# Another stated instruction order for attention and the first MLP, with the ring place of every tile stated

## The chip, the cores and the metric

The kernel runs on one core of one Trainium2 chip. The metric is device time in microseconds (us), the median of several executions. A profile is one execution recorded by the hardware; its span is shorter than its time by what lies around it. Engines are named as in the profile: PE (TensorE matmul), PEld (its weight loads), DVE (VectorE), ACT (ScalarE), POOL (GpSimd) and SP (SyncE, which here issues all DMAs).

## The reference, cut to what matters

Three parts follow one another: attention over 4 x 8 heads with a memory term, an MLP with a squared ReLU, and an MLP with a softmax-weighted activation and a layer norm.

```python
# attention: B, H, S, D = 4, 8, 576, 64
scores = scale * q @ k.T; scores = where(causal, -1e9, scores); scores -= scores.max(-1)
a = exp(scores); a /= a.sum(-1) + 1e-9
local = a @ v
q_p = phi(q)                      # phi(x) = where(x > 0, x, exp(x) - 1) + 1
mem_out = (q_p @ M_prev) / (q_p @ z_prev + 1e-6)
g = 1 / (1 + exp(-beta))          # one number for each head
x = g * mem_out + (1 - g) * local # -> 2304 tokens x 512
# MLP 1: d_ff 2048
r = maximum(x @ w_in, 0); x = (s * r * r + b) @ w_out
# MLP 2: d_ff 1024
h = x @ w_in2; solu = h * softmax(h); out = (layernorm(solu) * g_ln) @ w_out2
```

## The kernel before, in words

**Attention** works on 16 units (u = 0 to 15), each a pair of heads of one batch. The class `Attention` has one method for each step:

- `load` (L323): DMAs of keys and queries (`kq`), `q`, `v`, and once per batch `zb` and `Mb`.
- `scores` (L406): the score products of a unit in four groups, chunks 0 and 1 together (`s{u}_0`), then 2, 3 and 4 (`s{u}_2`, `s{u}_3`, `s{u}_4`). The products at L421 use 64 rows and all 128 columns of the PE array, those of group 4 (L452) the full array. DVE then takes scores and mask, writes `pr` and the row maximum `mx` (L437), and ACT takes the exponential with its row sum (L404). The scores have one buffer (`ps_s`), so the next group waits until DVE has read the one before.
- `transposes` (L463): PE transposes `pr` into `pp` (L478), ACT writes it scaled to `pt` (L482), for chunk 4 to `ptl`.
- `phi`, `weigh`, `recip_t`, `phi_t` (L343 to L400): the memory term's factors, transposed on PE as `tr`, `tp` and `tq` (L384, L394, L398).
- `values` (L493): products with `v`. `po` (L513) takes `pt_0` and then `pt_1`, `pe` (L516) takes `ptl`; both use all 128 rows and 64 columns of the array. `Mb` products on the full array end both (L518, L519).

**The first MLP** is spread over attention. Four of its 16 blocks of hidden units run there as filler (`first_part`, L566): hidden products `h` at L532 to L534, in `hidden`, and output products `y` at L594 to L596, all on the full array. The other 12 blocks run behind attention (`second_part`, ten rounds, L737 to L739), and then the second MLP (`mlp2`). Weights arrive as raw 8-byte numbers (`raw`, L246) and are decoded by ACT and DVE.

**What sets the order.** The text of the program gives a first order. `state_order` (L101) chains the instructions of each engine by the table `ORDER`, whose entries are indices into the program's text order, with `a+n` for a run of n. So each engine's queue from the start of the program to the first rounds of `second_part` is stated by hand; behind the stated part the order is that of the framework's scheduler. `load_gate` (L176) loads `beta` and makes `gate`, `omg` and `gmt` (ACT at L178, DVE at L179 to L185); `load_consts` (L187) loads `s_sb`, `b_sb` and `gl_sb`. `warm_up` (L170) issues products of zeros.

**Tiles.** A pool with `bufs=n` is a ring of n buffers for each tag. Before, the framework chooses which place of the ring a tile takes.

Of the kernel before, what the change touches and what calls it, by code (L numbers as in the profile page):

```python
# [15 lines left out]
PSUM = bass.MemoryType.PSUM  # L16
# [7 lines left out]

ORDER = {
    "PE": """
# [26 lines left out]
""",  # L53
    "Activation": """
# [15 lines left out]
""",  # L70
    "DVE": """
# [16 lines left out]
""",  # L88
    "Pool": """
3 15 17 5 11 0 13 2 6 12 8 10 14 16 20 18+2 23 21+2 26 24+2 29 27 32 28 30 35 31 33+2 38 36+2 41 39+2 44 42+2 47  # L90
45+2 50 48+2 53 51+2 56 54+2 59 57+2 60+2
""",
    "SP": """
# [3 lines left out]
""",  # L97
}


def state_order(tc):  # L101
    traced = {}
# [13 lines left out]
def attention_mlp_kernel(  # L116
# [76 lines left out]
    FP1 = 4  # L193
# [749 lines left out]
```

## Time and profile before

| | us |
|---|---|
| time, median of 3 runs (829.14 to 829.52) | 829.26 |
| the profiled execution: time | 829.67 |
| the profiled execution: span | 827.5 |
| PE busy in the span | 814.1 |
| ACT busy | 551.9 |
| DVE busy | 533.7 |
| POOL busy | 117.2 |

Read it like this: the profiled execution took 2.17 us more than its span and 0.41 us more than the median. Matmuls are pipelined and their ends are modelled, so on PE the distance from one start to the next tells more than the busy time of one instruction. The x in a timeline row counts hardware records: at L421, L452 and L513 to L519 one product of the program is two records, elsewhere it is one.

### The profile page before, as it was taken

The page shows a single profiled execution, that of the slowest core. Times are in us where ns is not written, and L with a number is a line of the kernel's source. Part 1 is how long each engine was busy: PE and PEld are TensorE (multiplying, and loading weights), DVE is VectorE, ACT ScalarE, POOL GpSimd, SP SyncE. Part 2 cuts the span into 40 slices and gives each one's busy share as a digit, 9 for nine tenths or more (in the row PEclk, how much of TensorE's full clock was granted, in tenths as well). Part 3 has the DMA queues.
Part 4 walks back from the last instruction along what each step waited for, and adds up shares of the span by engine and source line. Part 5 has one row for each costly group of instructions (what it writes and reads, how often), then busy time and mean ns, then how long its engine had stood idle before and what let it go on. Part 6 is the DMA issues. An engine that isn't in the chain of part 4 may idle for free.

```text
span 827.5 us, 13276 instructions
## 1 busy us (share of the span) xinstructions
PE 814.1 (98%) x4930; PEld 656.9 (79%) x4930; DVE 533.7 (64%) x1305; ACT 551.9 (67%) x1134; POOL 117.2 (14%) x124
## 2 busy tenths in 40 slices
PE   8999999999999999999999999999999999999997
PEld 6777777777777688888898888889887888888875
DVE  4999977978766566544566425454789665566552
ACT  6998878879778747666577656666865444445432
POOL 3221111111211100000000200030112233332000
PEclk9999999999999999999999999999999999999999
DMA  8342744343642025721132302211210000000001
GB/s 256 130 158 73 249 139 146 133 140 130 213 153 69 36 89 196 271 77 51 51 129 101 103 1 77 65 37 61 71 48 0 26 27 26 13 27 26 26 24 40
DMA packets 39759, 76.35 MB, mean 92 GB/s; under 512 B 6160, under 2 KB 16400, under 8 KB 39696
## 3 DMA queue, kind: packets, MB, share of 16 engines
q1 hardware_dynamic: 39696, 75.52, 27.2%
q8 instruction: 39, 0.64, 0.3%
q14 instruction: 24, 0.20, 0.1%
HBM read 61.35 MB, written 14.16 MB: 91 GB/s over the span
## 4 chain that ended last, share of the span: by engine, by line
PE 91%; DVE 4%; ACT 2%; DMA 1%; POOL 1%; issue 1%; SPq 0%; DVEq 0%; POOLq 0%
PE h L532 8%; PE h L533 8%; PE h L534 8%; PE y L738 6%; PE y L739 6%; PE y L737 6%; PE pp L478 5%; PE s L421 5%; PE o L871 4%; PE o L869 4%; PE o L870 4%; PE po L513 4%; PE y L596 2%; PE y L594 2%; PE y L595 2%; PE s L452 2%
## 5 line engine op out<-in xcount | busy, mean ns | idle before, releaser
L533 PE MATMUL h<-xl,w 128*128 128x512 f32 (+1 forms) x320 | 118.9, 372 | 0.0
L534 PE MATMUL h<-xh,w 128*128 128x512 f32 (+1 forms) x320 | 118.4, 371 | 0.0
L532 PE MATMUL h<-xh,w 128*128 128x512 f32 (+1 forms) x320 | 117.7, 378 | 0.0
L535 ACT ACTIVATE r<-h 128x512 f32<-128x512 f32 (+1 forms) x80 | 43.2, 553 | 90.6 <-PE h L534 87.8
L540 DVE TENSOR_TENSOR g<-r,g 128x512 fp32r<-128x512 f32 (+1 forms) x60 | 39.6, 665 | 83.4 <-ACT r L539 83.3
L738 PE MATMUL y<-g,w 128*128 128x512 f32 (+1 forms) x240 | 87.2, 368 | 0.0
L737 PE MATMUL y<-g,w 128*128 128x512 f32 (+1 forms) x240 | 87.2, 368 | 0.0
L404 ACT ACTIVATE pr<-pr,mx 128x512 f32<-128x512 f32 (+3 forms) x128 | 70.8, 555 | 16.1 <-DVE mx L437 15.6
L533 PEld LDWEIGHTS h<-xl,w 128*128 128x128 f32 x320 | 60.3, 189 | 10.8 <-DVE xl L562 1.1
L534 PEld LDWEIGHTS h<-xh,w 128*128 128x128 f32 x320 | 60.3, 189 | 10.2 <-DVE w L279 0.6
L532 PEld LDWEIGHTS h<-xh,w 128*128 128x128 f32 x320 | 59.7, 189 | 10.9 <-ACT r L535 0.6
L739 PE MATMUL y<-g,w 128*128 128x512 f32 (+1 forms) x240 | 66.6, 368 | 0.0
L437 DVE CUSTOM_DVE_ANT_0 pr<-s,big 128x128 f32<-128x128 f32 (+3 forms) x128 | 57.1, 487 | 14.5 <-PE s L421 12.6
L482 ACT ACTIVATE pt<-pp,omg 128x512 f32<-128x512 f32 (+3 forms) x128 | 60.1, 524 | 7.8 <-PE pp L478 7.3
L871 PE MATMUL o<-w,zl 128*128 128x512 f32 x144 | 56.6, 393 | 0.8 <-DVE var L847 0.8
L869 PE MATMUL o<-w,zh 128*128 128x512 f32 x144 | 56.7, 394 | 0.3 <-ACT zh L863 0.3
L870 PE MATMUL o<-w,zh 128*128 128x512 f32 x144 | 56.1, 390 | 0.0
L737 PEld LDWEIGHTS y<-g,w 128*128 128x128 f32 x240 | 45.3, 189 | 7.5
L421 PEld LDWEIGHTS s<-kq 64*128 64x128 f32 x640 | 39.7, 187 | 14.5 <-issue 7.2
L738 PEld LDWEIGHTS y<-g,w 128*128 128x128 f32 x240 | 45.2, 189 | 7.5
L478 PE MATMUL pp<-ident,pr 128*128 128x128 f32 x320 | 48.8, 276 | 2.2 <-ACT pr L404 2.1
L421 PE MATMUL s<-kq 64*128 64x128 f32 x640 | 48.6, 287 | 0.8 <-DVE mx L437 0.5
(165 smaller groups left out, 1855.7 us busy)
## 6 DMA issues: line engine op xcount, KB each, us to landing
raw<-in_moe_w_in_dram SPq DMA_DIRECT2D x24, 512.0 KB, 4.5
raw<-in_moe_w_out_dram SPq DMA_DIRECT2D x24, 512.0 KB, 3.7
kq<-in_kq_dram SPq DMA_DIRECT2D x16, 608.0 KB, 4.7
xr<-xd SPq DMA_DIRECT2D x8, 1024.0 KB, 5.4
q<-in_q_dram SPq DMA_DIRECT2D x16, 320.0 KB, 4.4
v<-in_v_dram SPq DMA_DIRECT2D x16, 320.0 KB, 3.4
xd<-xb SPq DMA_DIRECT2D x4, 1152.0 KB, 5.0
out_dram<-os SPq DMA_DIRECT2D x18, 256.0 KB, 2.0
```

The lines of the kernel that those rows point to most:

```text
L404: mark[0] = nc.scalar.activation(pr, pr, AF.Exp, bias=mx, scale=-1.0, accum_out=sm).ins
L421: self.last = nc.tensor.matmul(ss[:, j, c0 + k * P:c0 + (k + 1) * P], x[:, S + i * P:S + (i + 1) * P], x[:, k * P:(k + 1) * P], start=True ...
L478: nc.tensor.transpose(pp[:, e * n + c * P:e * n + (c + 1) * P], pr[:, c * P:(c + 1) * P], ident)
L532: nc.tensor.matmul(ps, wc[0], xh[:, c, 0:n], start=(c == 0), stop=False)
L533: nc.tensor.matmul(ps, wc[0], xl[:, c, 0:n], start=False, stop=False)
L534: nc.tensor.matmul(ps, wc[1], xh[:, c, 0:n], start=False, stop=(c == NC - 1))
L737: nc.tensor.matmul(o, wc[0], gh[:, 0:n], start=(f == fs[0]), stop=False)
L738: nc.tensor.matmul(o, wc[1], gh[:, 0:n], start=False, stop=False)
L739: nc.tensor.matmul(o, wc[0], gl[:, 0:n], start=False, stop=(f == fs[-1]))
L869: nc.tensor.matmul(oo, zh, w[:, 0], start=(f == 0), stop=False)
L870: nc.tensor.matmul(oo, zh, w[:, 1], start=False, stop=False)
L871: nc.tensor.matmul(oo, zl, w[:, 0], start=False, stop=(f == NF2 - 1))
```

## The change

`ORDER` is replaced by another table for all five engines. It states more of the program: on PE up to text index 2088 (1799 before), on ACT 545 (484), on DVE 632 (584), on SP 153 (144). New are a table `SLOTS` and a class `Slots`, which wraps the pools of attention and of the first MLP. A wrapped pool makes one tag for each place of the ring, with one buffer, and the table states the place of each tile in turn; the number of buffers stays. Every engine issues the same instructions as before. Line numbers of the kernel after are 50 or 51 higher from `load_gate` on.

```diff
 ORDER = {
     "PE": """
-0+30 46 34+6 47 40 62+4 41+5 30+4 68+3 48+8 71+3 56+6 102+3 66 80+7 67 87 105+2 74+6 107+7 88 92+5 89+3 126+6 97 101
+0+27 28+5 46 34+6 27 62+4 47+9 40 68+2 71+3 70 33 56+2 66 80+4 41+2 67 84+4 58+3 74+6 88+4 43+2 92 45 93+4 102+12
...
     "SP": """
-17+13 32 34 38 46+2 30+2 41 33 35+2 43 51 37 39+2 54 42 45 44 57 48 50 69+2 60 49 52+2 63 55+2 58 71 64 66 76 61 73
+17 27+2 20 23 18 24 22 21 32 19 25 34 30 38 26 31 41 33 36 43 35 51 54 37 40 47 39 57 45 44 48 52 42 60 53 46 63 50
...
+SLOTS = {
+    "kq": "0101010101010101",
...
+    "t": ("012012120201020120120212012020120202102112021202012021201022012202012121220021201012010121012012"
...
+class Slots:
+    def __init__(self, pool, name=""):
+        self.pool, self.name, self.turn = pool, name, {}
+
+    def tile(self, shape, dtype, tag=None, **k):
+        places = SLOTS.get(f"{self.name}{tag}")
+        if places:
+            n = self.turn[tag] = self.turn.get(tag, -1) + 1
+            k["bufs"] = 1
+            tag += "_" + (places[n] if n < len(places) else str(n % (int(max(places)) + 1)))
+        return self.pool.tile(shape, dtype, **({"tag": tag} if tag else {}), **k)
...
-            pool = lambda name, bufs, **k: actx.enter_context(tc.tile_pool(name=name, bufs=bufs, side="right", **k))
+            pool = lambda name, bufs, **k: Slots(actx.enter_context(
+                tc.tile_pool(name=name, bufs=bufs, side="right", **k)))
...
-        gs = pctx.enter_context(tc.tile_pool(name="gs", bufs=FP1 + 1))
+        gs = Slots(pctx.enter_context(tc.tile_pool(name="gs", bufs=FP1 + 1)), "gs.")
...
-        ps_m = fctx.enter_context(tc.tile_pool(name="ps_m", bufs=2, space=PSUM))
+        ps_m = Slots(fctx.enter_context(tc.tile_pool(name="ps_m", bufs=2, space=PSUM)), "ps_m.")
```

The next listings are rows of the engines' queues: line, operation, out<-in, shape, and how many stand in a row. Numbers behind the last underscore of a name only keep tiles apart.

PE, unit 4, before. Its value products begin with `pt4_0`, between two score groups of unit 5 with transposes and MLP products around:

```order
L421 MATMUL s5_0_1131<-kq5_908 128x128 x6
L513 MATMUL po4_1224<-pt4_0_1056,v4_822 64x256 x2
L513 MATMUL po4_1224<-pt4_0_1056,v4_822 64x128 x2
L519 MATMUL pe3_991<-mq3_971,Mb0_133 128x64
L394 MATMUL tp4_1176<-ident_58,ph4_1047 128x128
L398 MATMUL tq4_1182<-ident_58,ph4_1047 128x128
L421 MATMUL s5_2_1254<-kq5_908 128x128 x6
L478 MATMUL pp4_8_1214<-ident_58,pr4_t_1089 128x128
L490 MATMUL ppu4_1220<-ident_58,pr4_t_1089 128x128
L478 MATMUL pp4_8_1214<-ident_58,pr4_t_1089 128x128 x3
L394 MATMUL tp4_1176<-ident_58,ph4_1047 128x128 x3
```

Some rows later the others follow, behind the next score group:

```order
L421 MATMUL s5_3_1303<-kq5_908 128x128 x8
L516 MATMUL pe4_1225<-ptl_137,v4_822 64x64 x10
L513 MATMUL po4_1224<-pt4_1_1109,v4_822 64x256 x6
L513 MATMUL po4_1224<-pt4_1_1109,v4_822 64x128 x2
L594 MATMUL y0_1_1752<-g0_2_1428,w6_1128 128x512
L595 MATMUL y0_1_1752<-g0_2_1428,w6_1128 128x512
```

PE, unit 4, after:

```order
L541 MATMUL ppu4_1220<-ident_58,pr4_t_1089 128x128
L472 MATMUL s5_2_1254<-kq5_908 128x128 x6
L567 MATMUL pe4_1225<-ptl_137,v4_822 64x64 x9
L564 MATMUL po4_1224<-pt4_0_1056,v4_822 64x256 x2
L564 MATMUL po4_1224<-pt4_0_1056,v4_822 64x128 x2
L564 MATMUL po4_1224<-pt4_1_1109,v4_822 64x256 x6
L564 MATMUL po4_1224<-pt4_1_1109,v4_822 64x128 x2
L567 MATMUL pe4_1225<-ptl_137,v4_822 64x64
L472 MATMUL s5_3_1303<-kq5_908 128x128 x8
L645 MATMUL y0_0_1613<-g0_0_1197,w4_862 128x512
L645 MATMUL y0_1_1752<-g0_0_1197,w4_862 128x512
L569 MATMUL po4_1224<-mq4_1175,Mb1_134 128x512
```

All value products of unit 4 now stand in one row between `s5_2` and `s5_3`, where they stood at two places, and fewer products of the first MLP stand between the score groups.

SP at the start of the program, before (the DMAs in the order of their issue):

```order
L332 DMA kq0_139<-in_kq_dram 128x1216
L177 DMA gate_76<-in_beta_dram 128x8
L332 DMA kq1_166<-in_kq_dram 128x1216
L335 DMA q0_168<-in_q_dram 128x640
L338 DMA zb0_170<-in_z_prev_dram 128x512
L340 DMA Mb0_133<-in_M_prev_dram 64x4x64 x2
L335 DMA v0_174<-in_v_dram 128x640
L335 DMA q1_185<-in_q_dram 128x640
L335 DMA v1_187<-in_v_dram 128x640
L188 DMA s_sb_79<-in_moe_s_dram 128x1
L189 DMA b_sb_80<-in_moe_b_dram 128x1
L191 DMA gl_sb_81<-in_moe2_g_ln_dram 128x8x1
```

After:

```order
L383 DMA kq0_139<-in_kq_dram 128x1216
L238 DMA s_sb_79<-in_moe_s_dram 128x1
L239 DMA b_sb_80<-in_moe_b_dram 128x1
L386 DMA q0_168<-in_q_dram 128x640
L391 DMA Mb0_133<-in_M_prev_dram 64x4x64
L227 DMA gate_76<-in_beta_dram 128x8
L386 DMA v0_174<-in_v_dram 128x640
L391 DMA Mb0_133<-in_M_prev_dram 64x4x64
L389 DMA zb0_170<-in_z_prev_dram 128x512
L296 DMA raw0_324<-in_moe_w_in_dram 128x4x256
L383 DMA kq1_166<-in_kq_dram 128x1216
L386 DMA q1_185<-in_q_dram 128x640
```

The load of `gate` moves from the second place to the sixth, behind two constants, `q0` and the first half of `Mb0`.

ACT at the start, before (`pr0_0_0` and its like are the exponentials of unit 0's first score group):

```order
L178 ACT_TABLE_LOAD
L178 ACTIVATE gate_76<-gate_76 128x8
L404 ACTIVATE pr0_0_0_201,sums0_199<-pr0_0_0_201,mx_202 128x128
L404 ACTIVATE pr0_0_1_204,sums0_199<-pr0_0_1_204,mx_205 128x128
L404 ACTIVATE pr0_1_1_212,sums0_199<-pr0_1_1_212,mx_213 128x256
L404 ACTIVATE pr0_1_0_209,sums0_199<-pr0_1_0_209,mx_210 128x256
```

After:

```order
L455 ACT_TABLE_LOAD
L455 ACTIVATE pr0_0_0_201,sums0_199<-pr0_0_0_201,mx_202 128x128
L228 ACTIVATE gate_76<-gate_76 128x8
L455 ACTIVATE pr0_1_0_209,sums0_199<-pr0_1_0_209,mx_210 128x256
L455 ACTIVATE pr0_0_1_204,sums0_199<-pr0_0_1_204,mx_205 128x128
L455 ACTIVATE pr0_1_1_212,sums0_199<-pr0_1_1_212,mx_213 128x256
```

The exponential of `gate` moves behind the first of the four, and ahead of the other three.

DVE at the start, before (rows with `mx` are the second half of L437's instruction):

```order
L179 TENSOR_SCALAR gate_76<-gate_76 128x8
L180 RECIPROCAL gate_76<-gate_76 128x8
L183 COPY gmt_78<-gate_76 64x4
L184 COPY gmt_78<-gate_76 64x4
L185 TENSOR_SCALAR gmt_78<-gmt_78 128x4
L437 ISA pr0_0_0_201,mx_202<-s0_0_192,big_63 128x128
L437 ISA mx_202 128x1
L437 ISA pr0_0_1_204,mx_205<-s0_0_192,big_63 128x128
L437 ISA mx_205 128x1
```

After:

```order
L488 ISA pr0_0_0_201,mx_202<-s0_0_192,big_63 128x128
L488 ISA mx_202 128x1
L488 ISA pr0_0_1_204,mx_205<-s0_0_192,big_63 128x128
L488 ISA mx_205 128x1
L488 ISA pr0_1_0_209,mx_210<-s0_0_192,big_63 128x256
L488 ISA mx_210 128x1
L488 ISA pr0_1_1_212,mx_213<-s0_0_192,big_63 128x256
L488 ISA mx_213 128x1
L229 TENSOR_SCALAR gate_76<-gate_76 128x8
```

The reductions of unit 0's first score group now stand ahead of the operations on `gate`.

## Rows read from the trace of the kernel before

**Rows 1.** Page, busy time of each engine: us, share of the span, instructions.

```profile
PE 814.1 (98%) x4930; PEld 656.9 (79%) x4930; DVE 533.7 (64%) x1305; ACT 551.9 (67%) x1134; POOL 117.2 (14%) x124
```

**Rows 2.** Busy time by stretch: stretch, length, engines, granted clock, DMA share, GB/s.

```profile
20.00:75.00 55.00, 54.52 (x489) 40.28 (x487) 51.78 (x166) 51.86 (x133) 11.32 (x10) 1.00 0.41 140
75.00:290.00 215.00, 212.83 (x1739) 161.42 (x1738) 163.06 (x493) 174.63 (x426) 35.07 (x33) 1.00 0.41 136
...
330.00:630.00 300.00, 300.00 (x1459) 253.79 (x1458) 168.34 (x290) 199.95 (x338) 19.27 (x18) 1.00 0.24 80
```

**Rows 3.** Waits of PE, 0 to 300, behind the start: who for whom, us in total, times, longest.

```profile
PE tr L384 <- ACT r L374: 0.7, 1, 0.7
PE pe L516 <- ACT ptl L488: 0.6, 1, 0.6
PE s L421 <- DVE mx L437: 0.5, 2, 0.3
PE s L452 <- DVE xb L521: 0.3, 1, 0.3
PE s L452 <- DVE mx L437: 0.2, 1, 0.2
```

**Rows 4.** Timeline of PE, 78 to 92.5: start, us, operation, records.

```profile
80.34 0.39 PE L533 MATMUL h<-xl,w 128*128 128x512 f32 x1
80.56 0.40 PE L534 MATMUL h<-xh,w 128*128 128x512 f32 x1
80.89 0.94 PE L421 MATMUL s<-kq 64*128 64x128 f32 x12
...
87.83 0.80 PE L516 MATMUL pe<-ptl,v 128*64 128x64 f32 x20
88.46 1.69 PE L513 MATMUL po<-pt,v 128*64 128x256 f32 x16
```

**Rows 5.** Timeline of PE, 99 to 109.

```profile
105.80 0.80 PE L516 MATMUL pe<-ptl,v 128*64 128x64 f32 x20
106.53 0.50 PE L594 MATMUL y<-g,w 128*128 128x512 f32 x1
106.87 0.40 PE L595 MATMUL y<-g,w 128*128 128x512 f32 x1
```

**Rows 6.** Timeline of all engines, 0 to 13.

```profile
1.18 0.42 SPq L177 DMA_DIRECT2D gate<-in_beta_dram  x1
...
2.12 0.43 SPq L335 DMA_DIRECT2D q<-in_q_dram  x1
...
2.59 0.45 SPq L338 DMA_DIRECT2D zb<-in_z_prev_dram  x1
...
3.08 2.18 SPq L340 DMA_DIRECT2D Mb<-in_M_prev_dram  x2
...
4.65 0.94 PE L421 MATMUL s<-kq 64*128 64x128 f32 x12
...
6.46 0.21 ACT L178 ACTIVATE gate<-gate 128x8 f32<-128x8 f32 x1 [4.45 <-DMA gate<-in_beta_dram]
...
7.66 0.29 DVE L437 CUSTOM_DVE_ANT_0 pr<-s,big 128x128 f32<-128x128 f32 x1
...
8.39 0.39 ACT L404 ACTIVATE pr<-pr,mx 128x128 f32<-128x128 f32 x1
```

**Rows 7.** DMA issues, 0 to 3: engine, count, KB, median us to landing.

```profile
q<-in_q_dram SPq DMA_DIRECT2D x1, 320.0 KB, 7.2
zb<-in_z_prev_dram SPq DMA_DIRECT2D x1, 256.0 KB, 7.6
gate<-in_beta_dram SPq DMA_DIRECT2D x1, 4.0 KB, 5.3
```

**Rows 8.** Line L340 (loads of Mb): us from issue to landing.

```profile
DMA to landing us min/median/max: 2.3/4.7/7.7
```

**Rows 9.** DVE groups by shape, 0 to 300: us busy, mean ns, idle before.

```profile
L437 DVE CUSTOM_DVE_ANT_0 pr<-s,big 128x512 f32<-128x512 f32 x32 | 21.0, 685 | 3.2 <-PE s L421 2.0 <-ACT mq L396 0.9
```

More of the change, by code (lines that the diff above doesn't have):

```diff
@@ L26 @@
     "PE": """
[26 rows of a table removed]
[32 rows of a table added]
 """,
     "Activation": """
[15 rows of a table removed]
[17 rows of a table added]
 """,
     "DVE": """
[16 rows of a table removed]
[19 rows of a table added]
 """,
     "Pool": """
-3 15 17 5 11 0 13 2 6 12 8 10 14 16 20 18+2 23 21+2 26 24+2 29 27 32 28 30 35 31 33+2 38 36+2 41 39+2 44 42+2 47
-45+2 50 48+2 53 51+2 56 54+2 59 57+2 60+2
+3 6 10 15 11 5 13 17 0 8 2 12 14 16 18+4 23 22 26 24+2 27 29 28 30 32 31 33+2 36 35 38 37 39 41 40 42+3 47 45+2 48+2
+51 50 53 52 54 56 55 57+5
 """,
     "SP": """
[3 rows of a table removed]
-""",
-}
[4 rows of a table added]
+""",
+}
+SLOTS = {
+    "kq": "0101010101010101",
+    "ps_m.m": "0101010101010101010101010101010101010",
+    "q": "0101010101010101",
+    "v": "0101010101010101",
+    "den": "0123401234012340",
+    "sums": "0101010101010101",
+    "pr0": "01010101010101010101010101010101",
+    "mx": ("012340213402134023140231432130412303142301423041234023124013402131024310243014203142034130241302"
+           "0243102434013241032023104231012430230413240132401324301243004301"),
+    "pr1": "01010101010101010101010101010101",
+    "pr2": "01101010101010101010101010100101",
+    "t": ("012012120201020120120212012020120202102112021202012021201022012202012121220021201012010121012012"
+          "100210012100121212012012012212012211202102102101021021021100210210120102102210210102012021201022"),
+    "pr3": "01010110101010101010101010101010",
+    "sm": "0123401234012340",
+    "gs.r": "01101001010101010101010010101010",
+    "gs.g": "01234012340123401234012340123401",
+    "ys.y": "01101110101001101010",
+    "ps_h.h": "01010101010101010101",
+}
+class Slots:
[8 more added lines that the diff above has]
+        return self.pool.tile(shape, dtype, **({"tag": tag} if tag else {}), **k)
 def state_order(tc):
@@ L629, in attention_mlp_kernel @@
         xs = pctx.enter_context(tc.tile_pool(name="xs", bufs=1))
-        gs = pctx.enter_context(tc.tile_pool(name="gs", bufs=FP1 + 1))
+        gs = Slots(pctx.enter_context(tc.tile_pool(name="gs", bufs=FP1 + 1)), "gs.")
         xp = fctx.enter_context(tc.tile_pool(name="xp", bufs=2))
-        ys = fctx.enter_context(tc.tile_pool(name="ys", bufs=2))
-        ps_m = fctx.enter_context(tc.tile_pool(name="ps_m", bufs=2, space=PSUM))
+        ys = Slots(fctx.enter_context(tc.tile_pool(name="ys", bufs=2)), "ys.")
+        ps_m = Slots(fctx.enter_context(tc.tile_pool(name="ps_m", bufs=2, space=PSUM)), "ps_m.")
         fpools = [ys, [ps_m]]
@@ L689, in attention_mlp_kernel @@
         ps_y = pctx.enter_context(tc.tile_pool(name="ps_y", bufs=1, side="right", space=PSUM, reuse_waits="tile"))
-        ps_h = pctx.enter_context(tc.tile_pool(name="ps_h", bufs=2, side="right", space=PSUM, reuse_waits="tile"))
+        ps_h = Slots(pctx.enter_context(tc.tile_pool(name="ps_h", bufs=2, side="right", space=PSUM, reuse_waits="tile")), "ps_h.")
         fpools[1] = [ps_h, ps_m]
```

128 rows, old and new, of the table ORDER are left out of this document.

## The prediction

> **What bounds the kernel now.** I read the busy times first: PE is busy 98% of the span [rows 1]. The stretches then say where anything but PE could matter [rows 2]. From 330 to 630 us PE is busy 300.00 of 300.00 us, and from 75 to 290 us 212.83 of 215, while ACT and DVE have nearly a fifth or more free there. Only from 20 to 75 us are all three nearly full: PE 54.52, ACT 51.86 and DVE 51.78 of 55 us. The granted clock is 1.00 in each of these rows, which is the level of 2.4 GHz, so no time is to be had from the clock. The waits of PE behind the start add up to 0.7 + 0.6 + 0.5 + 0.3 + 0.2 = 2.3 us [rows 3]. So an order of instructions can gain little by ending waits. It can gain by making PE's own work shorter, and it can lose wherever it lets PE arrive before its data.
>
> The changed order ends early in the program: behind the third round of `second_part`, about 410 us, all five queues read alike in both kernels. Whatever the change does, it does before that.
>
> **PE's own work: changes of the array's shape.** PE works in three forms: 64 rows by 128 columns for the scores at L421 (call it A), 128 by 64 for the value products at L513 and L516 (B), and the full array (C) for all else. A change between them costs time that counts as busy. An MLP product starts 0.22 us behind another one (80.34 to 80.56), but the first score product starts 0.33 us behind the last MLP product (80.56 to 80.89): 0.11 us to go from C to A [rows 4]. The ten `pe` products (20 records) take 0.63 us up to a `po` product of the same form (87.83 to 88.46) [rows 4], and 0.73 us up to an MLP product (105.80 to 106.53) [rows 5]: 0.10 us to leave B. The MLP product that comes first behind B is slow too: 0.34 us to the next start (106.53 to 106.87) instead of 0.22, another 0.12 us [rows 4, 5]. A full exit from B thus costs 0.22 us.
>
> Counted along the two queues of PE (program rows, attention and first MLP), the changes of form fall from 160 to 126. Runs of A stay 48. Runs of B fall from 51 to 31, since `pt_0`, `pt_1` and `ptl` products now mostly stand together, as the listing of unit 4 shows, so 20 exits from B go: 20 x 0.22 = 4.4 us. Entries from C into A or B fall from 61 to 47: 14 x 0.11 = 1.5 us. Against this, 8 runs of A that went straight into B now go back into C, and the slow first product behind them, 0.12 us each, is new: +1.0 us. The sum is -4.4 - 1.5 + 1.0 = -4.9 us. Its ends: without the slow first products 20 x 0.10 + 14 x 0.11 = -3.5 us; without the payment for A into C -5.9 us. I take -4.9, because both parts have a row of their own. About a quarter, 1.1 us, lies before 75 us, where ACT and DVE are nearly as full as PE and could absorb it; I don't take it off, because PE is the fullest of the three in that stretch too [rows 2].
>
> **PE's waits behind the start.** Five waits, 2.3 us in all [rows 3], are what could be won. For most pairs of producer and consumer the new queue puts more PE work between them: counted with PE's start distances, the work between the first score group of a unit and its first transposes grows from a median of 6.7 to 8.4 us, between `pp` and the `po` products of `pt_1` from 1.5 to 2.95, between `tp` and the `Mb` products from 3.1 to 4.7. For `ptl` (0.6 us of wait) it stays at 1.8. For the score buffer it shrinks: between groups 3 and 4 from 2.6 to 2.05 us, between group 4 and the next unit's first from 2.5 to 1.5. So some of the waits go and some could grow. I take half of what `tr` and `pe` cost, (0.7 + 0.6) / 2 = 0.65 us, as gained; ends: all gone, -2.3, and as much again, +2.3.
>
> **The start.** The load of `gate` goes from second to sixth on SP, and ACT's exponential of `gate` stands ahead of three of the first four exponentials. So ACT blocks there until `gate` has landed (G), and behind it wait those three exponentials, on PE the transposes that need them, and on DVE everything from the `gate` operation on. Before, `gate` was issued at 1.18 and landed 5.3 us later [rows 7], ACT took it up at 6.46, and the second exponential began at 8.39 [rows 6]. After, it begins about 0.25 us behind G, so by ACT the start is even at G = 8.1. G early: SP comes to it after the first half of `Mb0`, about 4.3 (two halves issue from 3.08 for 2.18 us [rows 6]), and the shortest landing of such a load, 2.3 us [rows 8], makes it 6.6. G late: landings come in the order of issue. `kq0` was there at 4.65, when the first scores began, and `gate` 1.8 us behind it [rows 6]; `q0` landed at 2.12 + 7.2 = 9.3 and `zb0` at 2.59 + 7.6 = 10.2, 0.9 us apart [rows 6, 7]. With 1.8 us for each of two constants and `gate`, and 0.9 for `q0` and `Mb0`, G = 4.65 + 3 x 1.8 + 2 x 0.9 = 11.85. By ACT that is between -1.5 and +3.7 us, +1.1 in the middle. On DVE the reductions of the first scores no longer wait for `gate`: the scores were done at 4.65 + 0.94 = 5.6, the first reduction began at 7.66 [rows 6], so they gain up to 2.0 us, and with them PE's second score group. I take 0, between +1.1 and +1.1 - 2.0 = -0.9.
>
> The Trainium skill, page "DMA: Bandwidth & Descriptors", section "Anatomy of one DMA — SWDGE (gpsimd) path", gives a fixed cost of about 2.0 us for one DMA (told there for another issuing path). An estimate by that page is a landing of `gate` at 4.3 + 2.0 = 6.3, the start 1.8 us better and the whole at -7.35, 821.9. The row above speaks against it here: `gate`, 4 KB, took 5.3 us as the second load.
>
> **The ring places.** The number of buffers is the same, no instruction is added, and no wait for a free place stands among PE's waits [rows 3]. I take 0; the ends are covered by those of the waits.
>
> **The sum.** -4.9 - 0.65 + 0 = -5.55 us against the profiled execution's 829.67 gives 824.1. The median of the runs is 0.41 below that execution, so the forecast is 823.7.
>
> **Rivals.**
>
> 1. Start and waits gain as well. `gate` lands early, DVE's lead counts, and all waits go: -4.9 - 2.0 - 2.3 = -9.2, 820.1 on the median's footing. For it: most of the work between producers and consumers grows. Against: landings in the order of issue. Chance 0.12.
>
> 2. `gate` lands late. -5.55 + 3.7 = -1.85, 827.4. For it: five loads stand ahead of it and the first landings are 0.9 to 1.8 us apart. Against: two of the five carry one number each. Chance 0.11.
>
> 3. PE's gain is waited away where ACT and DVE are full. PE comes to the first scores of unit 4 with 7 fewer MLP products behind it (11 for 18), to those of unit 5 with 16 fewer (32 for 48), 16 x 0.22 = 3.5 us earlier. ACT and DVE have 3.1 and 3.2 us free in 55 [rows 2]. If none of their work moves back with it, PE waits 3.5 us there and the 1.1 us before 75 us are absorbed too: -4.9 + 1.1 + 3.5 = -0.3, 829.0. Against: the same table puts weight decoding later on ACT and DVE as well. Chance 0.13.
>
> 4. Slower, by the score buffer. DVE needs two reductions of 685 ns to free it behind group 3 [rows 9], 1.4 us, with 2.05 us of PE work in the median and 1.1 at the least to cover them; behind group 4 the cover is 1.5 us. If PE waited at each of the 32 places as long as at the longest such wait before, 0.3 us [rows 3], it would be 9.6 us: -5.55 + 9.6 = +4.05, 833.3. It becomes slower than before by over 0.2% from (5.55 + 1.66) / 32 = 0.23 us a place. Against: places with as little cover existed before, and cost 0.5 + 0.2 us in all. Chance 0.12.
>
> 5. The table doesn't do what it says. The queues of the built kernel differ as described, so this is left 0.02 and time 829.3.
>
> **How the numbers follow.** The forecast has 0.50. A measurement of this kernel can tell about 0.2%, 1.66 us, from no change: faster is below 827.6, slower above 830.9. Faster: the forecast, rival 1, two thirds of rival 2, which lies at the bound, and a small part of rival 3: 0.50 + 0.12 + 0.07 + 0.03 = 0.72. Same: the rest of rivals 2 and 3, and rival 5: 0.04 + 0.10 + 0.02 = 0.16. Slower: rival 4, 0.12. The range leaves out rival 4, and reaches from rival 1 with the far end of the changes of form (-5.9 for -4.9), 819.1, to rival 3 with their near end (-3.5 for -4.9), 830.4.
>
> **What would show it right or wrong.** In the profile of the changed kernel PE's busy time should fall by 4 to 6 us, all of it before 300 us, with the same number of instructions; from 330 to 630 us PE should again be full, and the MLP part behind it should have the same length. The value products should stand as one run of records in most units. PE's waits behind the start should stay near 2 us. ACT's wait for `gate` and the landing of that load show the start's term: the second exponential at 8 to 9.5. I am wrong if PE's waits grow by several us on `mx` (rival 4) or on `pr` and `r` between 40 and 90 us (rival 3), or if PE's busy time doesn't fall, which would mean that the price of a change of form isn't what I read from single rows.

## The result and the profile after

The changed kernel takes 819.94 us (819.77 to 820.10), the one before 829.20 beside it: a ratio of 0.9888, 95% interval 0.9870 to 0.9905. That is 9.3 us faster. All times here are medians over executions in the fast state; one slow execution each of tidy2 and best1 is left out. The forecast was 823.7 with a range of 819.1 to 830.4, so the direction is right, the time lies near the lower end of the range, and the gain is 1.7 times the forecast's 5.5 us.

The page of the kernel after, its span and its busy times:

```profile
span 818.1 us, 13268 instructions
...
PE 806.3 (99%) x4930; PEld 657.9 (80%) x4930; DVE 527.6 (64%) x1305; ACT 548.7 (67%) x1134; POOL 115.3 (14%) x124
```

PE is busy 7.8 us less than before [rows 1], with the same number of instructions, and idle 818.1 - 806.3 = 11.8 us for 13.4. So five sixths of the gain is work of PE itself that became shorter, and one sixth is idle time.

The stretches of the kernel after (columns as in [rows 2]):

```profile
0.00:8.00 8.00, 6.86 (x49) 4.94 (x51) 2.02 (x13) 2.67 (x7) 4.21 (x16) 1.00 0.62 182
8.00:20.00 12.00, 11.03 (x103) 8.20 (x101) 10.30 (x38) 11.60 (x31) 2.81 (x2) 1.00 0.94 319
20.00:75.00 55.00, 54.00 (x509) 42.41 (x506) 52.64 (x171) 52.28 (x135) 10.51 (x12) 1.00 0.44 147
75.00:290.00 215.00, 213.96 (x1756) 167.24 (x1755) 159.91 (x492) 174.62 (x430) 34.04 (x33) 1.00 0.39 129
...
330.00:620.00 290.00, 290.00 (x1414) 245.28 (x1413) 164.59 (x285) 194.19 (x330) 18.75 (x17) 1.00 0.24 83
```

and the two first ones of the kernel before, which were not shown:

```profile
0.00:8.00 8.00, 5.51 (x36) 3.71 (x36) 1.36 (x10) 1.50 (x3) 4.19 (x16) 1.00 0.54 186
8.00:20.00 12.00, 11.29 (x102) 8.41 (x103) 7.98 (x36) 10.77 (x31) 2.85 (x3) 1.00 1.09 296
```

Idle time of PE is a stretch's length less the first busy time. In the first 20 us it falls from 2.49 + 0.71 = 3.2 to 1.14 + 0.97 = 2.1 us. From 20 to 290 us it falls from 0.48 + 2.17 = 2.65 [rows 2] to 1.00 + 1.04 = 2.04 us. Behind that PE is full up to the second MLP, as before: from 409 us on in the kernel before, 400 in the kernel after, the same products start 9.5 us apart up to the end. Together that is -1.1 - 0.6 us of idle time and -7.8 us of busy time, 9.5 of the 9.4 us that the span fell.

PE's waits in the kernel after, 0 to 290 us (who for whom, us in total, times, longest):

```profile
...
PE s L503 <- DVE mx L488: 1.0, 2, 0.8
PE s L503 <- DVE mx L506: 0.6, 1, 0.6
PE tr L435 <- ACT r L425: 0.4, 2, 0.2
PE s L472 <- DVE mx L488: 0.3, 1, 0.3
PE pe L567 <- ACT ptl L539: 0.2, 1, 0.2
```

Against [rows 3], `tr` (0.7) and `pe` (0.6) wait 0.4 and 0.2 us now. The waits for the score buffer (`mx`) grew behind the start from 0.7 to 1.0 us, one of them 0.8 us long. The unit that the prediction looked at, on PE's timeline:

```profile
80.19 0.94 PE L472 MATMUL s<-kq 64*128 64x128 f32 x12
81.06 0.74 PE L567 MATMUL pe<-ptl,v 128*64 128x64 f32 x17
81.58 0.43 PE L564 MATMUL po<-pt,v 128*64 128x256 f32 x1
81.63 0.22 PE L567 MATMUL pe<-ptl,v 128*64 128x64 f32 x1
81.69 2.33 PE L564 MATMUL po<-pt,v 128*64 128x256 f32 x23
83.79 0.28 PE L567 MATMUL pe<-ptl,v 128*64 128x64 f32 x2
84.00 1.16 PE L472 MATMUL s<-kq 64*128 64x128 f32 x16
```

The value products of unit 4 stand in one run from 81.06 to 84.00, between two score groups. Before, they stood at two places, at 81.75 (below) and from 87.83 on [rows 4]:

```profile
81.75 0.87 PE L513 MATMUL po<-pt,v 128*64 128x256 f32 x8
```

Now there is one entry into their form and one exit.

The start, on the timeline of all engines:

```profile
3.57 0.59 SPq L227 DMA_DIRECT2D gate<-in_beta_dram  x1
...
6.09 0.29 DVE L488 CUSTOM_DVE_ANT_0 pr<-s,big 128x128 f32<-128x128 f32 x1 [5.09 <-PE s L472]
...
7.11 0.21 ACT L228 ACTIVATE gate<-gate 128x8 f32<-128x8 f32 x1 [0.19 <-DMA gate<-in_beta_dram]
...
7.23 0.49 ACT L455 ACTIVATE pr<-pr,mx 128x256 f32<-128x256 f32 x1
```

The load of `gate` is issued at 3.57 as the sixth and ACT takes it up at 7.11, 0.65 us later than before. The first reduction begins at 6.09 for 7.66 and the second exponential at 7.23 for 8.39 [rows 6].

### The profile page after: what moved, and what is told of

The parts are those of the page before. It is cut to its first block, busy times and chain, and to the rows that moved or that the text cites. A ratio compares the mean times of both kernels' runs of the same rounds, so it can differ in the third digit from the quotient of the medians.

```text
span 818.1 us, 13268 instructions
## 1 busy us (share of the span) xinstructions
PE 806.3 (99%) x4930; PEld 657.9 (80%) x4930; DVE 527.6 (64%) x1305; ACT 548.7 (67%) x1134; POOL 115.3 (14%) x124
## 4 chain that ended last, share of the span: by engine, by line
PE 91%; DVE 4%; ACT 2%; POOL 1%; DMA 1%; issue 1%; SPq 0%; POOLq 0%; ACTq 0%
PE h L583 8%; PE h L585 8%; PE h L584 8%; PE y L788 6%; PE y L789 6%; PE y L790 6%; PE pp L529 5%; PE s L472 4%; PE o L922 4%; PE o L920 4%; PE o L921 4%; PE po L564 3%; PE y L647 2%; PE y L646 2%; PE y L645 2%; PE s L503 2%
## 5 line engine op out<-in xcount | busy, mean ns | idle before, releaser
L455 ACT ACTIVATE pr<-pr,mx 128x256 f32<-128x256 f32 (+3 forms) x128 | 71.0, 557 | 12.4 <-DVE mx L488 12.0
L584 PEld LDWEIGHTS h<-xl,w 128*128 128x128 f32 x320 | 60.4, 189 | 10.3 <-DVE xl L613 0.7
L583 PEld LDWEIGHTS h<-xh,w 128*128 128x128 f32 x320 | 60.1, 189 | 10.3 <-issue 0.2
L533 ACT ACTIVATE pt<-pp,omg 128x256 f32<-128x256 f32 (+3 forms) x128 | 60.9, 522 | 7.5 <-PE pp L529 7.4
```

What stands on the lines that cost most here:

```text
L455: mark[0] = nc.scalar.activation(pr, pr, AF.Exp, bias=mx, scale=-1.0, accum_out=sm).ins
L583: nc.tensor.matmul(ps, wc[0], xh[:, c, 0:n], start=(c == 0), stop=False)
L584: nc.tensor.matmul(ps, wc[0], xl[:, c, 0:n], start=False, stop=False)
```

## The experiments

Where an experiment changes an order, its diff shows rows of the engine's queue (out<-in, shape, how many in a row). The time of the kernel after is 819.9 throughout, that of the kernel before 829.2 to 829.3 beside the runs.

### What a change of the array's form costs

**wedge** puts products of the first MLP into runs of value products of the kernel after:

```diff
 MATMUL h1_0_2183<-xh1_2171,w0_332 128x512
+MATMUL pe7_1921<-ptl_137,v7_1482 64x64 x2
 MATMUL h1_1_2301<-xh1_2171,w1_467 128x512
+MATMUL pe7_1921<-ptl_137,v7_1482 64x64 x4
 MATMUL h1_1_2301<-xl1_2172,w1_467 128x512
-MATMUL pe7_1921<-ptl_137,v7_1482 64x64 x10
+MATMUL pe7_1921<-ptl_137,v7_1482 64x64 x4
```

> The kernel after with 23 products of the first MLP, which stand 1 to 14 rows ahead of a run of value products, put into the middle of that run (one or two for each of 14 runs): changes of the array's form rise from 126 to 174, each moved product comes at most about 2 us later, and no attention product is moved away from its partners. If changes of form carry the gain, PE's own work grows by 8.3 us by the prices fitted to both traces and the time is 828.2. If the 28 us of the kernel with the value products split were lost to waits alone and a change of form costs next to nothing, it stays within 1 us of 819.9.

Measured: 832.5 us (831.1 to 832.8), 12.6 more than the kernel after and above both expectations; the profiled execution stands at the lower end. Its page, and the place of the diff on PE's timeline:

```profile
span 829.2 us, 13268 instructions
...
PE 815.3 (98%) x4930; PEld 658.7 (79%) x4930; DVE 527.3 (64%) x1305; ACT 548.5 (66%) x1134; POOL 115.2 (14%) x124
```

```profile
142.73 0.34 PE L568 MATMUL pe<-ptl,v 128*64 128x64 f32 x4
143.00 0.50 PE L584 MATMUL h<-xh,w 128*128 128x512 f32 x1
143.43 0.45 PE L568 MATMUL pe<-ptl,v 128*64 128x64 f32 x8
143.81 0.49 PE L585 MATMUL h<-xl,w 128*128 128x512 f32 x1
144.24 0.45 PE L568 MATMUL pe<-ptl,v 128*64 128x64 f32 x8
144.62 0.94 PE L473 MATMUL s<-kq 64*128 64x128 f32 x12
```

The two MLP products start 0.43 us before what follows them (143.00 to 143.43, 143.81 to 144.24), where 0.22 us is their distance within a row of their like [rows 4], and four value products between them take 0.38 us (143.43 to 143.81), where ten in one row take 0.63. PE's busy time grows by 815.3 - 806.3 = 9.0 us for 24 more runs of value products, 48 changes of form: 0.375 us a run. That is near the 8.3 expected. The rest of the 11.1 us in the span is idle time, with longer waits than in the kernel after:

```profile
PE pe L568 <- ACT ptl L540: 2.0, 1, 2.0
PE s L504 <- DVE mx L489: 1.7, 2, 0.9
```

So a change of form costs PE's own time. How much of the change's 7.8 us that explains depends on what is counted: the 20 runs of value products that it took away are worth 7.5 us at 0.375 a run, the 34 changes of form 6.4 us at 0.19 a change. wedge adds one kind only (from C to B and back), the change takes away several kinds, so wedge's price alone doesn't settle it.

The two traces do, counted place by place from 20 to 345 us. For each record (a product, or half of one) take the distance to the next start, without idle time, and subtract the median distance of records of the same shape in a row of their like, over both traces. At the changes of form (the last record ahead of one and the first three behind it) this excess adds up to 29.4 us before and 22.1 after, 7.3 less; at all other records it is 7.1 and 7.3 us. So what fell is the time at changes of form, and nothing fell elsewhere but the 0.6 us of idle time. With two to five records taken behind each change, the fall at the changes is 7.3 to 7.5 us; with only one, which cuts a product of two records in half, it is 4.7.

The Trainium skill, page "TensorEngine Tiling (Array Packing)", section "Key Properties", says that a change of the tiling mode drains the engine. The trace agrees in that each change costs time, 0.19 us on average in wedge; that this time is a drain, no run here shows.

**split** takes the products of `pt_1` away from those of `pt_0` in the kernel after, to just ahead of the `Mb` product:

```diff
 MATMUL po_399<-pt_0_253,v_174 64x256 x2
 MATMUL po_399<-pt_0_253,v_174 64x128 x2
-MATMUL po_399<-pt_1_313,v_174 64x256 x6
-MATMUL po_399<-pt_1_313,v_174 64x128 x2
 MATMUL s_2_429<-kq_166 128x128 x6
...
+MATMUL po_399<-pt_1_313,v_174 64x256 x6
+MATMUL po_399<-pt_1_313,v_174 64x128 x2
 MATMUL po_399<-mq_379,Mb_133 128x512
```

> The kernel after with the value products of pt_1 moved away from those of pt_0, to just ahead of the Mb product, in all 16 units: changes of the array's form rise from 126 to 153, nothing else is touched. If changes of form carry the gain, PE's own work grows by 4.0 us by prices fitted to both traces, and the time is 823.9. If the gain comes from ended waits instead, the time stays within 1 us of 819.9.

Measured: 848.3 us, 28.4 more (843.1 to 849.5; the lowest, 23.1 more, is the one execution at a granted clock of 1.00 throughout). Neither expectation holds: 4 us of form were expected, and the waits were not. On DVE and on ACT, 20 to 300 us:

```profile
DVE xb L571 <- PE po L569: 16.7, 10, 3.1
```

```profile
ACT pt L533 <- PE po L564: 5.1, 2, 3.4
```

DVE waits 16.7 us for the value products where it multiplies them into `xb` (3.1 us in the kernel after), and what stands behind it in its queue, the reductions of later score groups among them, waits too. ACT waits 5.1 us to write `pt` while PE still has to read it. Some of the time is the clock's: behind some of PE's waits the granted clock of the profiled execution fell, to 0.91 on average from 40 to 60 us. A move on PE alone, of a few us, thus costs several times what it moves, since the queues of the others stand as they were.

**grouped** does one part of the change alone, in the kernel before: `pt_0` products move behind, to those of `pt_1`.

```diff
 MATMUL pp8_4_2056<-ident_58,pr8_2_0_1969 128x128 x2
-MATMUL po8_2141<-pt8_0_1986,v8_1720 64x256 x2
-MATMUL po8_2141<-pt8_0_1986,v8_1720 64x128 x2
 MATMUL h1_3_2499<-xl1_2172,w3_728 128x512
...
 MATMUL tq8_2117<-ident_58,ph8_1977 128x128
+MATMUL po8_2141<-pt8_0_1986,v8_1720 64x256 x2
+MATMUL po8_2141<-pt8_0_1986,v8_1720 64x128 x2
 MATMUL po8_2141<-pt8_1_2055,v8_1720 64x256 x6
```

> The kernel before with one part of the change alone: in 15 of the 16 units the value products of pt_0 are moved behind, to stand with those of pt_1; changes of form fall from 160 to 137, all other engines keep their order. By forms alone PE's work falls by 3.9 us, to 825.4. If the other engines' queues rest on the old place, as in the kernel with the value products split, PE waits for them (the buffer of pt_0 comes free later) and the time is that or above 829.3.

Measured: 838.9 us, 9.8 slower than before: ratio 1.0117, interval 1.0101 to 1.0133. Page, and PE's waits from 20 to 300 us:

```profile
span 837.4 us, 13272 instructions
...
PE 813.6 (97%) x4930; PEld 659.4 (79%) x4930; DVE 534.3 (64%) x1305; ACT 552.3 (66%) x1134; POOL 117.0 (14%) x124
```

```profile
PE tr L382 <- ACT r L372: 3.5, 2, 3.0
PE s L419 <- DVE mx L435: 3.2, 6, 0.8
PE s L419 <- DVE sm L457: 1.3, 1, 1.3
```

PE is idle 837.4 - 813.6 = 23.8 us for 13.4, and busy only 0.5 us less although 23 changes of form are gone. But behind the wait of 3.0 us for `r` its granted clock fell, to 0.83 on average from 280 to 300 us, and in part of that stretch to 0.50:

```profile
288.00:290.00 2.00, 2.00 (x11) 1.43 (x11) 0.28 (x1) 1.26 (x2) 0.00 (x0) 0.50 0.00 0
```

20 us at 0.83 are worth (1 - 0.83) x 20 = 3.4 us of work at the full clock. That is an estimate, and an upper one, since PE was idle in part of them; without it PE would be busy up to 3.9 us less, as expected by forms. The count of excess at the changes of form gives 3.8 us less (25.6 for 29.4). So the forms paid here too, and the waits took more than they gave: `tr` and the score groups wait longer than before. This part of PE's new order, alone, doesn't bring the gain. That the orders of ACT and DVE, which were changed with it, keep the waits from growing is the likely reading, but not shown: no run exchanges the queues of single engines between the two tables, and which of their moves matters is open.

### Is the rest an end of waits?

In **light_before** and **light_after** both kernels have less to do on ACT and DVE, and the same on PE. Exponentials cover the last 128 columns (288 in the tail group), three decoding steps 64 of 512 columns, and the split of `x` is scaled with its low part zero:

```diff
-                mark[0] = nc.scalar.activation(pr, pr, AF.Exp, bias=mx, scale=-1.0, accum_out=sm).ins
+                d = pr[:, -(288 if pr.shape[1] == S else 128):]; mark[0] = nc.scalar.activation(d, d, AF.Exp, bias=mx, scale=-1.0, accum_out=sm).ins
...
-        nc.vector.tensor_tensor(a, a, lf, ALU.add)
+        nc.vector.tensor_tensor(a[:, 0:64], a[:, 0:64], lf[:, 0:64], ALU.add)
...
-            nc.scalar.activation(xh[:, c], x[:, c], AF.Copy)
-            nc.vector.tensor_tensor(xl[:, c], x[:, c], xh[:, c].bitcast(F32), ALU.subtract)
+            nc.scalar.activation(xh[:, c], x[:, c], AF.Copy, scale=1e-12)
+            nc.vector.tensor_tensor(xl[:, c], xh[:, c].bitcast(F32), xh[:, c].bitcast(F32), ALU.subtract)
```

> The kernel before with less work on ScalarE and VectorE and the same order and the same PE instructions: the exponentials cover only the last 128 columns of each row block (288 in the last group), three steps of the weight decoding cover 64 of 512 columns, and the split of x is scaled and its low part is zero. PE then waits less. If PE's waits behind the start in the kernel before come to about 8.7 us, as the start distances say, and not to the 2.3 us that the view of waits shows, the time falls by 5 us or more, to 824 or less. If only what the view shows can be won, it falls by at most 2.3, to 827.

> The kernel after with the same work left out. With waits gone on both sides, what remains between this and the kernel before with less work is PE's own work: 5.6 us by the prices of changes of form. If the 9.3 us of the change were changes of form alone, 9.3 us would remain. If it were waits alone, about 0.

Measured: 827.6 us (lowest 827.1) and 816.9 us (lowest 816.8), so 1.6 and 3.0 us less than with all the work, and 10.7 us apart (10.3 between the lowest). The stretch from 75 to 290 us of both, before first:

```profile
75.00:290.00 215.00, 213.64 (x1745) 162.50 (x1744) 149.84 (x493) 160.76 (x427) 34.54 (x33) 1.00 0.41 137
```

```profile
75.00:290.00 215.00, 214.72 (x1771) 169.32 (x1770) 147.40 (x488) 159.12 (x428) 32.21 (x32) 1.00 0.40 127
```

ACT and DVE are busy 12 to 16 us less from 75 to 290 us than with all the work, and the kernel before is hardly faster. What remains of PE's waits in it, 20 to 300 us:

```profile
PE tr L384 <- ACT r L374: 0.7, 1, 0.7
PE s L421 <- DVE mx L437: 0.5, 2, 0.3
```

The first expectation fell: I had read 8.7 us of short delays out of the distances between starts and taken them for waits that hide under the modelled ends of matmuls. If they were, less work on ACT and DVE should have ended at least some of them. By itself this is weak evidence, since the two waits above didn't end either. But the gap between the two kernels didn't shrink to 5.6 us, it stayed, and the count place by place above says the same: what the change gained lies in PE's own work. (The profiled execution of light_before ran from 8 to 20 us at a granted clock of 0.86, so only a stretch behind it is compared.)

### The start and the ring places

**gate_back** puts the chain of `gate` in the kernel after where it was, and **gate_moved** moves it in the kernel before as the change does. gate_moved does more than its expectation says: on SP the two constants, `q0` and the first half of `Mb0` go ahead of `gate`, and the second `kq`, 608 KB, goes behind it. In the queues of the kernel after, gate_back:

```diff
 SP:  kq0, 
+     gate, 
      s_sb, b_sb, q0, Mb0, 
-     gate, 
      v0, Mb0, zb0, raw0, kq1
 ACT: 
+     gate, 
      pr0_0_0, 
-     gate, 
      pr0_1_0, pr0_0_1, pr0_1_1
```

> The kernel after with only the gate's chain put back where it was: its load second on SyncE, its exponential first on ScalarE, its operations ahead of the first reductions on VectorE. If the start's lead of 2.25 us (first scores of unit 1 at 15.62 for 17.88) is owed to the gate's place and lives to the end, the time rises to about 822.1. If the lead is absorbed between 20 and 75 us, where all three engines are full, it stays at 819.9.

> The kernel before with only the gate's chain moved as the change does it: sixth load on SyncE, behind the first exponential on ScalarE, behind the first four reductions on VectorE. If that place alone brings the start's lead, 829.2 falls by about 2, to 827. If the lead needs the new order of all engines, the time stays near 829.2; if the later load hurts, it rises by up to 3.7.

Measured: gate_back 819.95 us (819.93 to 820.05), no difference. gate_moved 828.67 us, 0.67 faster than the kernel before: ratio 0.9988, interval 0.9978 to 0.9997. The start of gate_back:

```profile
1.18 0.42 SPq L226 DMA_DIRECT2D gate<-in_beta_dram  x1
...
5.42 0.21 ACT L227 ACTIVATE gate<-gate 128x8 f32<-128x8 f32 x1 [3.40 <-DMA gate<-in_beta_dram]
...
6.62 0.29 DVE L487 CUSTOM_DVE_ANT_0 pr<-s,big 128x128 f32<-128x128 f32 x1
...
7.51 0.51 ACT L454 ACTIVATE pr<-pr,mx 128x256 f32<-128x256 f32 x1
```

With `gate` second the first reduction begins at 6.62 instead of 6.09 and the second exponential at 7.51 instead of 7.23, and no time is lost by it. In the old order the move gives two thirds of a us, together with the other moves on SP, in the new one nothing; the 2 us that were thought possible came in neither. The load in gate_back, second as before, lands after 4.2 us (issued 1.18, taken up 5.42) and not after 5.3. Two loads of half a KB are issued behind it there, and one of 608 KB in the kernel before; that this makes the difference was not tried.

**no_places** empties the table of ring places:

```diff
 SLOTS = {
-    "kq": "0101010101010101",
...
 }
```

> The kernel after with the table of ring places emptied: the new order of all engines stays, the framework chooses each tile's place again. If the places are worth nothing by themselves, the time stays at 819.9 within 0.5 us. If they carry what the forecast missed (823.7 foretold, 819.9 measured), it rises to about 823 and new waits for a free tile appear.

Measured: 819.87 us, the same. The ring places are worth nothing by themselves.

### Can it be bettered?

**tidy** and **tidy2** end more changes of form by swaps on PE alone, **best1** and **best2** move what waits longest in the kernel after. Two of tidy's rows, and one of best2's moves:

```diff
 MATMUL pp15_7_3658<-ident_58,pr15_3_1_3610 128x128 x4
+MATMUL tr15_3664<-ident_58,r15_3637 128x128 x4
+MATMUL tp15_3672<-ident_58,ph15_3567 128x128 x4
 MATMUL po15_3706<-pt15_0_3576,v15_3337 64x256 x2
...
-MATMUL s5_4_1340<-kq5_908 128x288
...
 MATMUL y0_0_1613<-g0_0_1197,w4_862 128x512
+MATMUL s5_4_1340<-kq5_908 128x288
```

> The kernel after with two small swaps on PE that end changes of form (unit 15's first value products behind its reciprocal's transposes, unit 0's second score group behind its neighbours), 126 to 122 changes: by forms 0.7 us less, 819.2; by waits anything from that to 820.5.

> The kernel after with twelve swaps on PE of a score group or value products with up to 2.2 us of neighbouring work, 126 to 107 changes of form: by forms 3.4 us less, 816.5. If PE's order rests on what ScalarE and VectorE have ready, moving score groups by up to 2 us starves them, and the time is 820 or more, with new waits at the swapped places.

> The kernel after with five local moves at its longest waits: a product of unit 5's last score group three rows later, the reciprocal's transposes of units 2, 5 and 11 behind neighbours of 0.4 to 0.5 us, and on VectorE unit 1's third reductions ahead of a product with R, with two MLP products moved on PE for it. The waits at these places add up to 2.2 us, so 817.7 if all end; 819.9 or more if they only move to the next row.

> The same with the four moves on PE alone, without VectorE's: waits of 1.3 us at these places, so 818.6 if all end, 819.9 or more if they only move on.

Measured: tidy 824.1 us (822.7 to 827.3), tidy2 843.6 (840.8 to 846.9), best1 820.7 (820.7 to 821.5), best2 819.6 (819.5 to 820.3). PE's waits in tidy, 0 to 290 us:

```profile
PE tr L434 <- ACT r L424: 2.2, 3, 1.8
PE pp L528 <- ACT pr L454: 1.5, 2, 1.0
```

The swap in unit 15 put `tr` 1.8 us ahead of its data, and the one at the start made `pp` wait 1.5 us. This profiled execution is the slowest of tidy's, its granted clock was 0.50 from 12 to 16 us; at a mean clock of 1.00 tidy took 822.7 and 823.0, still 2.8 more than the kernel after. tidy2 is 23.7 us slower for an expected gain of 3.4 by forms. best2 is not to be told from the kernel after, and in best1 the waits moved on. No version beats the kernel after.

## Why the prediction was right, and where it was short

**What bounds the kernel, and where the change acts:** right. PE's own work is what fell, all of it before 410 us; the part behind takes the same time, and the granted clock stays at 1.00.

**The price of the forms (-4.9):** the mechanism was right and the size was off. PE's busy time fell by 7.8 us. By the prediction's terms a run less was worth 4.9 / 20 = 0.245 us, though its own rows make a round trip 0.10 + 0.12 + 0.11 = 0.33, near the 0.375 of wedge. So it went wrong less in the prices than in the adding up. Counted by kind in the two traces (excess as above, 20 to 345 us), the exits from B to C gave 6.8 us (21 fewer, at 0.28 each before) where the prediction had 20 at 0.22, 4.4. The changes from A straight to B, 7 fewer in that stretch, gave 1.4 us; the prediction had put them at nothing. The entries from C gave 0.7 us instead of 1.5, the runs of A that now end in C took back 1.2, near the 1.0 foreseen, and three changes more from B to A another 0.3. The ends given for this term, -3.5 to -5.9, didn't hold what was measured: both came from the same few rows, and both left the changes from A to B out.

**The waits behind the start (-0.65):** right. Idle time from 20 to 290 us fell by 0.6 us, `tr` and `pe` gained about 0.7 and the score buffer lost 0.3.

**The start (0):** off by 1.1 us, by which the start's idle time fell. `gate` was taken up at 7.11, near the early end of 6.6, not in the middle of 6.6 and 11.85: the two constants ahead of it landed about 0.2 us apart, not 1.8 each. The lead of the start is not the place of `gate` alone: gate_back, with `gate` second again, is as fast as the kernel after, and gate_moved, which moves more than `gate`, won 0.7 us in the old order.

**The ring places (0):** right, by no_places.

**The rivals.** Rival 1 gave the measured time (820.1), but that is chance: it kept the forms at 4.9 us and had 4.3 us of ended waits and an early start on top, where idle time brought 1.7 us of the gain. Rivals 2 and 3 didn't come: PE's idle time from 20 to 75 us grew by 0.5 us, not by 3.5. Rival 4's wait is there, 1.0 us in two places, far from 0.23 us at each of 32. split, grouped and tidy2 show that orders which are slower than the kernel before by over 0.2% do exist.

## What to carry to other kernels

Where one engine is full, look first at what its own sequence costs: count changes of the array's form by kind, leave no kind out, and sum them over the whole trace, not from the few rows that show one of them. An order of instructions is a set of queues that fit each other; a good move on one queue alone, be it of half a us, can cost several times what it gains, so try it with the others moved along, and measure. And take a start distance that is longer than usual for a wait only when the view of waits, or a run with the supposed cause made smaller, says so.

## What the runs showed of the hardware

A round trip of PE from MLP products to value products and back cost 0.375 us beyond the work, on average over the 24 that wedge adds. That is more than the MLP product itself (0.22 us).

A gap on PE can cost its clock. The profiled execution of no_places took 823.41 us, 3.5 above its median; its stretches from 14 to 22 us (columns as in [rows 2], the granted clock is third from the end):

```profile
14.00:16.00 2.00, 0.14 (x2) 0.13 (x2) 1.54 (x7) 1.09 (x2) 0.39 (x1) 1.00 0.49 172
16.00:18.00 2.00, 2.00 (x9) 1.41 (x9) 1.87 (x7) 1.02 (x2) 1.26 (x1) 0.60 0.84 268
18.00:20.00 2.00, 2.00 (x15) 1.64 (x15) 0.76 (x3) 1.52 (x4) 0.00 (x0) 0.55 1.03 346
20.00:22.00 2.00, 2.00 (x22) 1.65 (x22) 1.65 (x8) 1.28 (x4) 0.00 (x0) 1.00 0.76 306
```

PE was busy 0.14 of 2 us from 14 to 16, and the granted clock was 0.60 and 0.55 in the next four, so near the lower level of 1.2 GHz (0.5), before it was 1.00 again. Of the 3.5 us, 1.9 are the gap itself. The kernel after is busy at least 1.8 of 2 us in each of these stretches and stayed at 1.00. Such a gap doesn't always cost the clock: in the profiled execution of the kernel before, PE waits 2.1 us for an exponential of unit 0, and the clock stays at 1.00 there and behind it:

```profile
6.00:8.00 2.00, 0.57 (x6) 0.27 (x3) 1.18 (x8) 0.22 (x2) 0.00 (x0) 1.00 0.92 364
```

How long a small load takes differs with its place: `gate`, 4 KB, took 5.3 us as the second load with 608 KB behind it (the kernel before), 4.2 as the second with two tiny loads behind it (gate_back), 4.2 as the sixth with 608 KB behind it (gate_moved), and 3.5 as the sixth with 320 KB behind it (the kernel after). What makes the difference was not tried.
